# One fused attention and SSM kernel, the same tasks issued in another searched order

## The chip, the cores and the metric

The kernel runs on one core of a Trainium2 chip. The metric is device microseconds of one execution. TensorE is called PE here, its weight loads PEld, VectorE DVE, ScalarE ACT, GpSimd POOL and SyncE SP, as in the profile.

## The reference

Two branches over the same input `x` of 2048 positions and 640 channels, mixed by a gate:

```python
g = sigmoid((x * gate_w).sum(-1, keepdims=True))
a = attention(x, wqkv, wo)     # 32 heads of 20; 8 keys a position, 2 apart, backwards; softmax over 8
b = ssm(x, A, B, C, dt, Dskip) # K[d,l] = Re sum_n C*dB*exp(dt*A*l), y = causal conv(K, x) + x*Dskip
return g * a + (1 - g) * b
```

The convolution is done by FFTs in the reference and by matmuls with constant tables in the kernel.

## The kernel before

All work is cut into tasks. `Plan.add` makes a list of them; each has a name, the engines that can do it (`P` PE, `A` ACT, `D` DVE, `S` SP's DMA queue, `G` POOL's DMA queue; `AD` means ACT or DVE), and what it depends on. There are two plans, `main` (1295 tasks) and `tail` (304). `Plan.order` reads a string of numbers: each is the step to the next task's index in the list, and a letter behind it chooses the engine where there is a choice. `Plan.emit` issues the tasks in this order and chains each engine's instructions in it, so that an engine never overtakes: a task that waits holds all that stand behind it on its engine or queue. Data dependencies, the reuse of buffers and semaphores are worked out from the program, whatever the order is.

The task names, in the order in which the work flows:

- Parameters: `wr`, `tau`, `lin_t1` and the like on DVE and ACT, `mk0` to `mk9` pieces, `sp0` to `sp9` their stores, then `L0` to `L9`: loads of the SSM parameters for the ten chunks of kernel taps (L732; `L0` half on SP, half on POOL).
- Input: `turn`/`tev` transpose `x` (L207, eviction L473 on ACT or L475 on DVE). `late0` to `late59` are the projections to q, k and v (L291), `lev` their evictions, `lst<sc><w>` the stores to DRAM of quarter `sc` (w: 0 q, 1 k, 2 v; L307).
- Attention in eight pieces of 256 positions: loads `qc`, `kc` (L330) and `vc` (L339), both on POOL; `prod` (DVE, L345) and `lg` (PE, L351) make logits; `max`, `neg`, `exp`, `sum`, `at` the softmax (`exp` on ACT needs the Exp table); `ast` and `asb` send the weights through DRAM on SP; `pv` (DVE, L415) and `gat` (PE, L422) apply them, `oT` evicts; `wo` (PE, L446) projects, `ga` evicts with the gate (ACT L455, DVE L457), `gaS` stores on SP.
- Kernel taps in ten chunks `c`, three units each: `arg` (PE, L767), `act` (ACT: Sin L782, Exp L784), `pq`, `pqb`, `pqc` (DVE, L804 and L806), `kmm` (PE, L822, many short matmuls), `fin<c>` evicts the chunk. After chunk 4 and chunk 9 the taps are expanded: `shift`, `own`, `other` on DVE, `move` and `near`, stores `xst`, loads `xld` (L904, on SP and POOL).
- First FFT stage: `f1`, `fu`, `fk` matmuls (L1266, L1285) and their evictions `f1e`, `fue`, `fke` (some `fke` in halves `h0`, `h1`). `fu` reads `Usb`, which `rows0` to `rows7` load on POOL (L970); between two of them POOL copies two elements into `pace` (L969) when the earlier has landed. The buffer of `Usb` is that of the projections' staging tile, so `rows0` waits until all `lst` of quarters 1 to 3 have landed. `gates` loads the gate (`omF`, L973).
- Tail: `fp`/`sp` second FFT stage, `ta`, `tc`, `Y` the product on DVE, `inv`/`cp` inverse, `yp` then `tt`+`mx` or `st` the last stage with the mix, `out` the stores.

The function tables: an ACT task with a table (`exp`, `ln`, `sin`, `atan`) behind one with another needs an `ACT_TABLE_LOAD`.

Of the kernel before, what the change touches and what calls it, by code (L numbers as in the profile page):

```python
# [38 lines left out]
def _attn_consts():  # L39
# [10 lines left out]


ORDER = {"main": (
# [41 lines left out]
), "tail": (  # L94
# [8 lines left out]
)}  # L103


# [1259 lines left out]
```

## Time and profile before

| | us |
|---|---|
| median of 3 runs (339.92 to 340.62) | 340.38 |
| profiled execution, first to last instruction | 339.6 |
| busy: PE, DVE, ACT, POOL | 289.5, 298.9, 290.2, 92.3 |

The profiled execution is given by its span, 339.6 us; the median of the runs stands 0.8 us above it. Busy times say how long an engine worked on something; a busy PE is not PE at its peak. The views used below: busy time of each engine in stretches; groups of instructions by line, engine and shape (busy time in all, mean ns of one, idle time before them and what ended it); waits (who waited for whom); and the timeline, one row an instruction or a few merged ones (start, duration, engine, line, operation, tiles out<-in).

### The profile page before, as it was taken

The page shows a single profiled execution, that of the slowest core. Times are in us where ns is not written, and L with a number is a line of the kernel's source. Part 1 is how long each engine was busy: PE and PEld are TensorE (multiplying, and loading weights), DVE is VectorE, ACT ScalarE, POOL GpSimd, SP SyncE. Part 2 cuts the span into 40 slices and gives each one's busy share as a digit, 9 for nine tenths or more (in the row PEclk, how much of TensorE's full clock was granted, in tenths as well). Part 3 has the DMA queues.
Part 4 walks back from the last instruction along what each step waited for, and adds up shares of the span by engine and source line. Part 5 has one row for each costly group of instructions (what it writes and reads, how often), then busy time and mean ns, then how long its engine had stood idle before and what let it go on. Part 6 is the DMA issues. An engine that isn't in the chain of part 4 may idle for free. (4 is left out here: it accounts for less than half of the span.)

```text
span 339.6 us, 12013 instructions
## 1 busy us (share of the span) xinstructions
PE 289.5 (85%) x5181; PEld 172.1 (51%) x5214; DVE 298.9 (88%) x407; ACT 290.2 (85%) x424; POOL 92.3 (27%) x119
## 2 busy tenths in 40 slices
PE   0699999999997899999999979669999899996760
PEld 0446544444453455455545444445765676665750
DVE  3999988789998799999899989786888979999982
ACT  1899737999997899999999998786976779998991
POOL 8603334041052161102137615621130000000053
PEclk9999999999998999999999999997999999999996
DMA  7997854378279781285738585982882336576056
GB/s 251 356 259 233 222 131 133 103 207 166 66 195 249 186 204 38 42 233 161 252 58 206 124 224 129 207 187 50 235 281 93 124 113 198 139 142 118 2 136 177
DMA packets 48949, 56.30 MB, mean 166 GB/s; under 512 B 25498, under 2 KB 40154, under 8 KB 48898
## 3 DMA queue, kind: packets, MB, share of 16 engines
q1 hardware_dynamic: 39928, 27.90, 31.2%
q0 software_dynamic: 8224, 27.04, 30.2%
q8 instruction: 40, 0.66, 0.8%
q10 hardware_dynamic: 746, 0.61, 0.5%
q14 instruction: 11, 0.09, 0.1%
HBM read 36.26 MB, written 19.27 MB: 164 GB/s over the span
## 5 line engine op out<-in xcount | busy, mean ns | idle before, releaser
L291 PE MATMUL tb<-bufA 128*128 128x512 bf16 x267 | 73.3, 389 | 5.0 <-issue 3.1
L782 ACT ACTIVATE big<-ar 128x740 bf16<-128x740 int16 (+1 forms) x72 | 56.1, 854 | 2.5 <-issue 1.2
L784 ACT ACTIVATE big<-ar 128x848 bf16<-128x848 f32 x60 | 50.3, 918 | 1.8 <-PE ar L767 1.8
L767 PE MATMUL ar<-Rarg,L 64*128 64x212 bf16 (+4 forms) x600 | 48.8, 253 | 3.5 <-ACT big L784 1.5
L345 DVE TENSOR_TENSOR prod<-qc,kc 128x2048 bf16<-128x2048 bf16 x40 | 47.8, 1218 | 4.2 <-PE lg L351 3.3
L415 DVE TENSOR_TENSOR pv<-vc,asb 128x2048 bf16<-128x2048 bf16 x40 | 48.2, 1217 | 0.9 <-PE tb L422 0.9
L291 PEld LDWEIGHTS <-bufA 128*128 128x128 bf16 x300 | 31.0, 122 | 28.0 <-issue 11.3
L822 PEld LDWEIGHTS <-pt 128*32 128x32 bf16 (+1 forms) x2560 | 25.8, 92 | 37.0 <-issue 34.4
L822 PE MATMUL kps<-qq,pt 128*32 128x21 bf16 (+1 forms) x2560 | 36.9, 173 | 8.0 <-issue 6.6
L804 DVE TENSOR_TENSOR pt<-big 128x1024 bf16<-128x1024 bf16 x48 | 33.3, 701 | 5.6 <-issue 2.0
L767 PEld LDWEIGHTS <-L 64*128 64x128 bf16 x600 | 20.6, 94 | 27.1 <-issue 23.4
L446 PE MATMUL tb<-wo_sb,oT 128*128 128x320 bf16 x160 | 28.6, 301 | 0.7 <-DVE ga L457 0.4
L1157 POOL DMA_DIRECT2D out_dram<-ot x14 | 7.7, 557 | 77.9 <-DVE ot L1139 77.9
L473 ACT ACTIVATE prj<-tb 128x512 bf16<-128x512 f32 x32 | 20.0, 632 | 8.8 <-PE tb L291 8.6
L422 PE MATMUL tb<-pv,ind 128*64 128x512 bf16 (+1 forms) x192 | 25.0, 363 | 2.5 <-issue 2.3
L473 ACT ACTIVATE sp_u<-fp 128x640 bf16<-128x640 f32 x31 | 23.9, 952 | 0.8 <-PE fp L1039 0.8
L473 ACT ACTIVATE sp_k<-fp 128x640 bf16<-128x640 f32 x29 | 22.6, 969 | 1.2 <-DMA PHX<-c_phi 1.0
L969 POOL COPY pace<-Usb 32x2 bf16<-32x2 bf16 x7 | 14.3, 2045 | 25.9 <-DMA Usb<-in_A_x_dram 25.9
L806 DVE TENSOR_TENSOR qq<-big 128x1344 bf16<-128x1344 bf16 x24 | 21.2, 883 | 0.0
L339 POOL DMA_DIRECT2D vc<-vS x16 | 11.9, 771 | 28.9 <-DVE pv L415 12.4
L1039 PEld LDWEIGHTS <-PHI 128*128 128x128 bf16 x160 | 15.5, 97 | 8.0 <-issue 1.0
L455 ACT ACTIVATE ga<-tb,g_sb 128x320 bf16<-128x320 f32 x26 | 13.8, 544 | 4.4 <-PE tb L446 3.0
(168 smaller groups left out, 562.4 us busy)
## 6 DMA issues: line engine op xcount, KB each, us to landing
vc<-vS POOLq DMA_DIRECT2D x16, 327.5 KB, 6.9
kc<-kS POOLq DMA_DIRECT2D x8, 337.5 KB, 6.1
xn<-in_A_x_dram SPq DMA_DIRECT2D x4, 640.0 KB
qc<-qS POOLq DMA_DIRECT2D x8, 320.0 KB, 5.9
gaS<-ga SPq DMA_DIRECT2D x8, 320.0 KB
Usb<-in_A_x_dram POOLq DMA_DIRECT2D x8, 320.0 KB, 5.1
gaF<-gaS SPq DMA_DIRECT2D x8, 320.0 KB
bufA<-in_A_wqkv_dram SPq DMA_DIRECT2D x3, 800.0 KB
```

The source lines that it names most:

```text
L291: nc.tensor.matmul(ppf, self.wq[:, which, kt, e::5], self.xT[:, c0 // 1024, kt, c0 % 1024:c0 % 1024 + SC], start=(kt == 0), stop=(kt == NK ...
L345: nc.vector.tensor_tensor(b[e][:], b["qc"][:, e, :].unsqueeze(1).to_broadcast([128, W, C]), win(b["kc"][:, e, :], 0, W, DIL, C), ALU.mult)
L415: nc.vector.tensor_tensor(o, vw, b["asb"][:].unsqueeze(2).to_broadcast(sh), ALU.mult)
L422: nc.tensor.matmul(b["op", e][64 * a:64 * a + 64, 0:n, :], ind[:, 32:96], b["pv", e][:, w, a, 0:n, :], start=(w == 0), stop=(w == 3), skip ...
L446: nc.tensor.matmul(apf[:, :320], b["oT"][:, e, i * 128:(i + 1) * 128], wo_sb[:, e, hf * 320:(hf + 1) * 320], start=(e == 0), stop=(e == 4))
L473: nc.scalar.activation(o, i, ACT.Identity)
L767: nc.tensor.matmul(ar[:, g2, a0:a0 + ncol], L[rows, sb, gv, l0:l0 + 128], R[rows, c0:c0 + ncol], start=True, stop=True, tile_position=(64 ...
L782: nc.scalar.activation(d_[:, :, s0 * QW:s1 * QW], ar[:].bitcast(I16)[:, :, 0:2 * (s1 - s0) * QW:2], ACT.Sin, scale=SCL)
L784: nc.scalar.activation(dst[:, gp::2].rearrange("p g s n -> p g (s n)"), ar[:, :, 0:2 * EW], ACT.Exp)
L804: nc.vector.tensor_tensor(pt[:, :, k, :], gg[:, :, ::-1] if k else gg, e1, ALU.mult)
L806: nc.vector.tensor_tensor(qq[:], trg[:, :, KI:].rearrange("p a (v m) -> p a v m", v=2), exq[:, :, KI:].unsqueeze(2).to_broadcast([128, 32, ...
L822: nc.tensor.matmul(kps[32 * g:32 * g + 32, h, NM * ql:NM * ql + NM], pt[rows, k, v, :], qq[rows, k, v, :], start=(g not in started), stop= ...
```

## The change

Both strings of `ORDER` are replaced; nothing else is. The title's search is the program that wrote the string; it is no part of the kernel. The diff, cut to the first and last numbers of each plan:

```diff
 ORDER = {"main": (
-    "52 -52 7 -4 -2 3 11 -4 -6 -3 51A -45 -2 6 48 1D -5 1A -44 41 1A 3 1A 13 -63 1 15 -2 61 -11 1D -60 2 69 1A -5 1 -4 1 "
...
+    "0 3 -1 4 1 1 1 1 5 10 -13 -11 3 24 1 29 1 -7 2 -1 2 5 -30 31 -5 1 15 1 11 -73 2 34 27 11 -80 83 -65 66 -3 4 1 1 -78 79 "
...
+    "-642 644 -1 -7 9D -8 15 1 -27 22 -21 11 11D -21 6 -5 6 4D 11 4 -24 25 -4D -19 -1 15 -13D 7 7 -37 31 -30"
 ), "tail": (
-    "3 1A 7 1A -7 1D 1 6 1A -6D 1 1A 10 -5 1A 1 1A 3 13 1D -13 1 1 2 1A 3 1A -3 1A -4 11 1A 6 -11 1A 11 -6 1A 1 1A -41 1 "
...
+    "3 -3 5 -1D 2D 5 1 -11 12 -11 5 1 7 -6 5D 3 21 -18 -4 -6D 11 13 -16 1 20 -13 9 -7 -1 9 -7 8 -15 1 7 -6 8 -1 -6 15 -7 20 "
```

Read against the list of tasks, the two orders differ as follows. Evictions that may run on either engine (DVE before, DVE after; the rest on ACT): `lev` 19, 17; `ga` 6, 11; `oT` 3, 6; `fue` 6, 2; `fke` 6, 5; `fin` 4, 2; `tev` 2, 1; `lin_t1` 0, 1; in the tail `sp` 4, 5. ACT's order in `main` changes its table 18 times before and 22 after; `exp0` and `exp3` now stand between Sin tasks of one chunk.

What stands ahead of `fin9`, the last chunk's eviction, and behind it in `main`, where the two orders differ:

| | ahead, before | ahead, after | behind, before | behind, after |
|---|---|---|---|---|
| DVE `pv` | 30 | 35 | 10 | 5 |
| DVE `ga`, `oT`, `lev` | 2, 0, 19 | 7, 3, 17 | 4, 3, 0 | 4, 3, 0 |
| DVE `fin`, `tev`, `lin_t1` | 3, 2, 0 | 1, 1, 1 | 0 | 0 |
| DVE `fue`, `fke`, `fke` halves | 0 | 0 | 6, 3, 3 | 2, 4, 1 |
| ACT table loads of the plan | 18 | 22 | 0 | 0 |
| ACT `fue`, `f1e` | 0, 9 | 6, 10 | 14, 1 | 12, 0 |
| ACT `ga`, `oT`, `lev` | 18, 16, 41 | 17, 17, 43 | 8, 5, 0 | 4, 1, 0 |
| ACT `fin`, `tev`, `lin_t1` | 6, 8, 1 | 8, 9, 0 | 0 | 0 |
| ACT `fke`, `fke` halves | 0 | 0 | 2, 7 | 1, 9 |

POOL's queue in the stretches that change most (each name waits for its data, and holds the ones behind it):

```
before: lst00 lst01 qc0 kc0 kc256 qc256 L0G lst11 consts kc512 lst10 ...
after:  lst00 lst01 kc0 qc0 qc256 L0G kc256 lst02 lst10 vc0 qc512 ...

before: ... xst0G lst22 rows0 rows1 qc1792 vc1024 rows2 kc1792 rows3 rows4 xld0G rows5 vc1280 rows6 vc1536 rows7 gates1 gates3 vc1792 xst1G ...
after:  ... xst0G xld0G lst32 lst22 rows0 vc1024 rows1 qc1792 kc1792 rows2 rows3 rows4 vc1280 rows5 rows6 rows7 gates3 gates2 gates1 gates0 vc1536 vc1792 xst1G ...
```

SP's queue, the main differences: `L2 ast1 asb0 L3 asb1` becomes `asb0 L2 ast1 L3 gaS0 asb1`; `L8 gaS1 ast4 asb4 L9 gaS2 ast5 xld0S` becomes `ast4 xld0S L8 ast5 gaS2 asb4 L9`; at the end of the tail the stores of the eight output pieces are issued in the order 1 0 2 3 4 7 6 5.

90 rows, old and new, of the table ORDER are left out of this document.

## The prediction

> **What bounds the kernel now.** First the page's head and busy shares, then the busy time of each engine in stretches cut where the work changes: loads and parameters, the projections, the joint stretch of attention and kernel chunks, the last chunk's end (`fin9` starts at 236.7), the end of the main plan (271.5), the tail.
>
> ```profile
> span 339.6 us, 12013 instructions
> PE 289.5 (85%) x5181; PEld 172.1 (51%) x5214; DVE 298.9 (88%) x407; ACT 290.2 (85%) x424; POOL 92.3 (27%) x119
> ...
> core 0: us, PE busy (x) PEld busy (x) DVE busy (x) ACT busy (x) POOL busy (x), PEclk, DMA share, GB/s
> 40.00:58.00 18.00, 17.09 (x104) 7.88 (x104) 15.16 (x23) 8.89 (x16) 5.94 (x9) 1.00 0.58 159
> 58.00:120.00 62.00, 57.00 (x1147) 27.81 (x1158) 54.34 (x73) 57.37 (x78) 15.73 (x20) 0.97 0.67 164
> 120.00:200.00 80.00, 74.16 (x1822) 39.35 (x1830) 77.12 (x108) 79.67 (x121) 28.96 (x31) 1.00 0.59 152
> 200.00:236.70 36.70, 29.93 (x808) 17.58 (x805) 30.59 (x40) 28.95 (x42) 13.21 (x17) 0.95 0.66 147
> 236.70:271.50 34.80, 32.12 (x248) 23.24 (x247) 30.62 (x43) 27.41 (x40) 3.84 (x7) 1.00 0.60 185
> 271.50:334.00 62.50, 51.59 (x832) 38.59 (x832) 57.61 (x88) 56.52 (x94) 7.07 (x13) 0.99 0.52 128
> ```
>
> No one engine is the bound. In 40 to 58 PE is (17.1 of 18), ACT idles 9.1. In 120 to 200 DVE and ACT are both full (77.1 and 79.7 of 80). In 200 to 236.7 ACT idles 7.8 and DVE 6.1, from 236.7 to 271.5 they idle 7.4 and 4.2: only there and in 40 to 58 is there slack that an order could take. The waits of 200 to 236.7 say why:
>
> ```profile
> PE kps L822 <- issue: 6.1, 4, 2.0
> ACT bufA L473 <- PE bp L1266: 3.2, 2, 2.7
> DVE pt L804 <- issue: 2.0, 1, 2.0
> ```
>
> PE stood 6.1 us in four waits for nothing but its own next instruction, amid the short `kmm` matmuls, and ACT and DVE then waited for PE.
>
> **The change part by part.** No task is added or dropped. Evictions change engine, ACT's order needs 22 switches of its function table instead of 18, and queues are permuted. I count what each engine has ahead of `fin9` and behind it, in both orders, and price the difference by these rows (busy, mean ns of one).
>
> ```profile
> L415 DVE TENSOR_TENSOR pv<-vc,asb 128x2048 bf16<-128x2048 bf16 x40 | 48.2, 1217 | 0.9 <-PE tb L422 0.9
> L473 ACT ACTIVATE big<-bp 128x1024 bf16<-128x1024 f32 x14 | 14.2, 1044 | 2.2 <-PE bp L1266 2.2
> L455 ACT ACTIVATE ga<-tb,g_sb 128x320 bf16<-128x320 f32 x26 | 13.8, 544 | 4.4 <-PE tb L446 3.0 <-ACT big L782 0.9 <-DMA gaS<-ga 0.4
> L475 DVE CAST big<-bp 128x1024 bf16<-128x1024 f32 x6 | 7.2, 1221 | 1.7 <-PE bp L1266 1.6
> L457 DVE TENSOR_SCALAR ga<-tb,g_sb 128x320 bf16<-128x320 f32 x6 | 3.2, 544 | 1.5 <-DMA gaS<-ga 1.3 <-PE tb L446 0.2
> L473 ACT ACTIVATE prj<-tb 128x512 bf16<-128x512 f32 x32 | 20.0, 632 | 8.8 <-PE tb L291 8.6
> L475 DVE CAST prj<-tb 128x512 bf16<-128x512 f32 x13 | 8.9, 686 | 3.5 <-PE tb L291 3.5
> L475 DVE CAST E<-kps 128x336 bf16<-128x336 f32 x4 | 2.0, 503 | 1.8 <-PE kps L822 1.8
> L782 ACT ACT_TABLE_LOAD x6 | 7.7, 1283 | 0.5 <-PE ar L767 0.4
> ```
>
> *Ahead of `fin9`, DVE*: 5 more `pv` (+6.1), 5 more `ga` (+2.7), 3 more `oT` (+1.8, priced as `prj` and a shorter one), 1 `lin` (+0.7, estimated as `prj`), 2 fewer `lev` (-1.4), 2 fewer `fin` (-1.0), 1 fewer `tev` (-1.2): +7.7. Successive instructions overlap: the pair of `pv` below takes 2.35, so the second adds 1.13, not 1.22. Nine net instructions at 0.08 less: **+7.0**. *ACT*: 4 table loads (+5.1), 6 more `fue` and 1 `f1e` (+7.3), 1 `tev` (+1.0), 2 `fin` (+1.0), 2 `lev` (+1.3), 1 `oT` (+0.6), less 1 `ga` and 1 `lin` (-1.6): +14.7, less 0.12 of overlap for twelve: **+13.2**. PE gains about 7 in matmuls of the same tasks; it had 6.8 idle in 200 to 236.7 alone and hides them. So `fin9` starts 7.0 later if DVE sets it (243.7) and 13.2 later if ACT does and fills no idle time (249.9). ACT can fill some: the loads around the first softmax (`exp0`, which now stands between two Sin tasks) fall at the end of the PE-bound stretch, about 1.5 of them in its 9.1 idle; the six `fue` stand in 200 to 236.7, where ACT idled 7.8, of which I take 3. That is 13.2 - 4.5 = 8.7: `fin9` at **245.4**.
>
> Here a rule weighs against the change. In the row each load takes 1283 ns with 0.5 us of idle time before all six, nothing like a second cost. The Trainium skill (ScalarE: Activation LUTs, "What ACT_TABLE_LOAD costs") adds a drain of about 1380 ns to each switch; by it four more switches would be 10.6 instead of 5.1 and the time at the end 343.3. The trace shows no such idle time, so the row decides, and that case gets 0.02 among the ACT-bound ones below.
>
> *Behind `fin9`, DVE*: 5 fewer `pv` (-6.1), 4 fewer `fue` (-4.9), 2 fewer half `fke` (-1.4), 1 more `fke` (+1.2): -11.2, with overlap **-10.3**. *ACT*: 4 `ga` (-2.2), 4 `oT` (-2.2), 2 `fue`, 1 `fke` and 1 `f1e` (-4.1) fewer, 2 halves more (+1.2): -7.3, with overlap **-6.0**. That leaves 20.3 on DVE and 21.4 on ACT of the 30.6 and 27.4 above. Then the chain from `fin9` through DRAM sets the end:
>
> ```profile
> 236.68 0.51 DVE L475 CAST E<-kps 128x336 bf16<-128x336 f32 x1 [1.76 <-PE kps L822]
> 239.59 0.76 DVE L869 COPY X<-nxt 128x80 bf16<-128x80 bf16 x3 [0.41 <-ACT nxt L473]
> 240.26 2.35 DVE L415 TENSOR_TENSOR pv<-vc,asb 128x2048 bf16<-128x2048 bf16 x2
> ...
> 246.15 0.56 POOL L904 DMA_DIRECT2D kc<-Kx  x1 [4.35 <-PE bp L1266]
> 248.71 0.38 SPq L904 DMA_DIRECT2D kc<-Kx  x1
> ...
> kc<-Kx POOLq DMA_DIRECT2D x2, 640.0 KB, 4.4
> ```
>
> `fin9` to the end of `other1` 3.7, plus one `oT` now between, 4.3; to the loads' issue 5.8 on POOL and 8.4 on SP (there `gaS5` stood ahead; now `gaS6` does), landing 4.4: 10.2 to 12.8, I take 11.5; then nine half `fke`, one whole and one `fue` on ACT, 6.5 with the first matmul. 22.3, against 21.4 of ACT work: **22.5**, or 27 if PE's ring waits cost again the 4 to 7 us idle of today. The tail has one `sp` eviction moved to DVE (0.7 either way) and its outputs reordered: 0, bounds 1 each way.
>
> *Queue positions.* On SP `asb0` moves ahead of `L2`, `xld0S` ahead of `L8`, and `gaS0` ahead of `asb1`. The first two wait for stores that are long issued when `L2` and `L8` may start. Behind `gaS0`, which waits for `ga011`, stand `asb1` and then `L4`; between `ga011` and the first `pv1` stand about seven `prod`-sized instructions of DVE, 8 us, for an issue and a landing: 0, bounds 0 and 2. On POOL two moves count. `kc256` moves behind the four `L0` loads:
>
> ```profile
> 47.63 2.59 POOL L732 DMA_DIRECT2D L<-Sprm  x4 [6.82 <-issue]
> ...
> 53.20 2.35 DVE L345 TENSOR_TENSOR prod<-qc,kc 128x2048 bf16<-128x2048 bf16 x2
> ...
> kc<-kS POOLq DMA_DIRECT2D x8, 337.5 KB, 6.1
> ```
>
> It was issued at 39; now at 50.2, landing at 56.3, while its `prod10` would start near 54.4 (two `lev` more ahead, one `prod` row as above): 0 to 1.9 lost in a PE-bound stretch; I take 1.0. The other is the rows chain, the first rival. *Renewals.* PE's waits for instructions (6.1) may shrink to nothing or be met elsewhere; bounds -6 and +6, taken 0, as the instructions and their number stay.
>
> **Sum.** The tail starts at 245.4 + 1.0 + 22.5 = 268.9 instead of 271.5: 339.6 - 2.6 = 337.0 of span. The median of the runs (340.38) stands 0.8 above this span: **337.8**. Bounds of the terms: 243.7 + 21 gives 333, 249.9 + 25 gives 343.
>
> **The rivals.** *First, the other side: the loads of the FFT's input come late.* `rows0` may start only when all projections are stored; the last eviction (`lev42`) now has 13.4 us more DVE work ahead (5 `prod`, 7 of the `pq` kind, 2 softmax pieces), so `rows0` is at 185.2.
>
> ```profile
> 171.76 0.80 POOL L970 DMA_DIRECT2D Usb<-in_A_x_dram  x1 [5.55 <-PE ar L767]
> 181.65 9.43 POOL L969 COPY pace<-Usb 32x2 bf16<-32x2 bf16 x1 [0.76 <-DMA Usb<-in_A_x_dram]
> 196.94 0.18 POOL L969 COPY pace<-Usb 32x2 bf16<-32x2 bf16 x1 [4.25 <-DMA Usb<-in_A_x_dram]
> 204.13 3.08 POOL L969 COPY pace<-Usb 32x2 bf16<-32x2 bf16 x1 [6.25 <-DMA Usb<-in_A_x_dram]
> 225.29 0.79 POOL L970 DMA_DIRECT2D Usb<-in_A_x_dram  x1
> 226.07 1.07 POOL L973 DMA_DIRECT2D omF<-omS  x2
> ...
> vc<-vS POOLq DMA_DIRECT2D x16, 327.5 KB, 6.9
> ```
>
> The eight loads took 53.5 from first to last issue, 11.7 of it two tiny pacing copies that took 9.43 and 3.08 (others about 0.4, 0.18 where DVE stood still). Without those 11.7 `rows7` is issued at 227.0, and `vc1536`, which stood ahead of it and now stands behind it and four small loads, lands 10.5 later (0.8 of its own issue, 2.1 of four `omF` loads, 0.7 of the first half, 6.9): 237.5. `pv60` has 1.1 more DVE work ahead than `fin9` had: 237.8. No margin is left. Held copies as in this trace make it 349 (337.8 + 11); half of them 343. It decides from 3.6 us of held copies on. For it: DVE stays nearly full there; against: ACT is the tighter engine there, and each DVE wait lets a copy through. By the Trainium skill (SBUF — State Buffer, "Who interferes with whom") a DVE instruction with two SBUF inputs blocks a GpSimd instruction that reads SBUF; the trace agrees (9.43 against 0.18).
>
> *Second, ACT becomes the bound*: nothing of the 13.2 is absorbed, 4.5 later: 342; with half absorbed 340.4, no change. *Third, the order removes the renewal stalls as well* (4 of the 6.1): 333.8. *Fourth, transfers and renewals were no cost and the orders are equal*: inside 340.4 ± 0.7.
>
> **How the numbers follow.** Forecast 337.8 (335.5 to 339.6): 0.42. Late rows, 341 to 349: 0.29. ACT-bound or equal, 339.7 to 343: 0.17, of which 0.13 within 0.2%. Better, 333 to 335.5: 0.12. This measurement tells a change from none at about 0.2% (0.7 us). Faster 0.42 + 0.12 = 0.54, same 0.13, slower 0.29 + 0.04 = 0.33. Range 333.0 to 346.0: it leaves out the far half of the late rows.
>
> **What would show it.** Right: 23 table loads on ACT, `fin9` near 245, the stretch from it to the tail's first `fp` 22 to 24 long, ACT idle in 40 to 58 below 9. Wrong: `pv60` waiting for `vc`, `fu8` waiting for `Usb` (rows chain); a first `fp` after 272; PE's instruction waits over 8 us.

## The result and the profile after

The changed kernel is not faster. In the first comparison it took 344.25 us (median of 4 executions, 342.08 to 345.49) beside 340.5 of the kernel before: a ratio of 1.0107 [1.0058, 1.0157]. Two later comparisons gave medians of 343.38 beside 342.6, ratio 1.0022 [0.997, 1.0073], and 342.6 beside 341.8, ratio 0.9901 [0.9844, 0.9957]. A ratio leaves disturbed executions out, and where few are left (three of twelve in the third comparison, four of thirteen for the changed main with the tail of before below) it can stand against its own medians. So means of all executions are given too. All 28 executions of the changed kernel have a mean of 342.8 us (standard error 0.5), 104 of the kernel before 342.2 (0.2): the difference is +0.2%, one to two standard errors, where -0.8% was forecast.

First the head of the page and the busy time in the same stretches as before (columns: us, then busy us and instructions of PE, PEld, DVE, ACT, POOL, the granted clock, DMA):

```profile
span 340.0 us, 12021 instructions
PE 287.1 (84%) x5188; PEld 174.5 (51%) x5214; DVE 296.4 (87%) x407; ACT 296.9 (87%) x428; POOL 89.4 (26%) x119
...
core 0: us, PE busy (x) PEld busy (x) DVE busy (x) ACT busy (x) POOL busy (x), PEclk, DMA share, GB/s
40.00:58.00 18.00, 16.14 (x164) 8.24 (x164) 15.11 (x23) 10.57 (x15) 5.53 (x8) 1.00 0.64 197
120.00:200.00 80.00, 69.20 (x1718) 37.58 (x1718) 72.77 (x105) 77.15 (x112) 18.97 (x28) 0.97 0.62 158
200.00:236.70 36.70, 33.67 (x895) 21.32 (x894) 31.85 (x40) 34.98 (x51) 19.62 (x19) 0.98 0.56 121
236.70:271.50 34.80, 29.65 (x279) 21.87 (x279) 26.71 (x40) 26.04 (x36) 2.82 (x5) 0.90 0.64 203
271.50:334.00 62.50, 50.90 (x824) 37.66 (x821) 57.96 (x87) 56.03 (x93) 6.00 (x11) 0.98 0.51 118
```

The slack of 200 to 236.7 and of 40 to 58 is used (ACT idles 1.7 instead of 7.8, and 7.4 instead of 9.1). But 120 to 200, full on DVE before (77.1), now has 72.8. The waits say why:

```profile
DVE pv L412 <- DMA vc<-vS: 4.4, 1, 4.4
DVE prod L342 <- DMA kc<-kS: 4.0, 1, 4.0
...
PE kps L819 <- issue: 0.5, 1, 0.5
```

PE's waits for its own instructions around 200 to 240 fell from 6.1 to 0.5 in this execution. In their place DVE waits twice for a load. The queue that issues these loads, POOL's:

```profile
180.30 0.81 POOL L967 DMA_DIRECT2D Usb<-in_A_x_dram  x1 [5.36 <-PE ar L764]
...
185.11 0.60 POOL L966 COPY pace<-Usb 32x2 bf16<-32x2 bf16 x1 [2.58 <-DMA Usb<-in_A_x_dram]
185.66 0.79 POOL L967 DMA_DIRECT2D Usb<-in_A_x_dram  x1
186.56 0.88 POOL L327 DMA_DIRECT2D qc<-qS  x1
187.42 0.88 POOL L327 DMA_DIRECT2D kc<-kS  x1
...
203.84 5.15 POOL L966 COPY pace<-Usb 32x2 bf16<-32x2 bf16 x1 [3.71 <-DMA Usb<-in_A_x_dram]
...
226.01 3.34 POOL L966 COPY pace<-Usb 32x2 bf16<-32x2 bf16 x1 [4.89 <-DMA Usb<-in_A_x_dram]
...
232.08 2.16 POOL L336 DMA_DIRECT2D vc<-vS  x3
```

and the DVE instructions that wait for them, with `fin9` (the eviction `E<-kps`) behind:

```profile
195.12 1.22 DVE L342 TENSOR_TENSOR prod<-qc,kc 128x2048 bf16<-128x2048 bf16 x1 [3.99 <-DMA kc<-kS]
...
239.15 3.50 DVE L412 TENSOR_TENSOR pv<-vc,asb 128x2048 bf16<-128x2048 bf16 x3 [4.45 <-DMA vc<-vS]
...
246.00 0.51 DVE L472 CAST E<-kps 128x336 bf16<-128x336 f32 x1 [0.62 <-PE kps L819]
```

`kc1792` is the `kc` issued at 187.42, behind `rows0`, its landing and `rows1`; its first `prod` (`prod70`) stands idle from 191.1 to 195.1. `vc1536` is among the three issued from 232.08 on.

The tail starts 1.5 us earlier than before and ends later: its own last part is longer. ACT's `tt` run breaks for 0.98 us and the last two `mx` come at its very end (after, then before):

```profile
321.59 2.20 ACT L1133 ACTIVATE tt<-yp,om 128x320 bf16<-128x320 f32 x5 [0.78 <-PE yp L1127]
324.77 7.21 ACT L1133 ACTIVATE tt<-yp,om 128x320 bf16<-128x320 f32 x17 [0.98 <-PE yp L1127]
...
332.21 1.05 DVE L1136 TENSOR_TENSOR ot<-tt,gaF 128x640 bf16<-128x640 bf16 x2
...
333.55 2.18 POOL L1154 DMA_DIRECT2D out_dram<-ot  x4 [1.42 <-DVE ot L1136]
```

```profile
323.00 9.30 ACT L1136 ACTIVATE tt<-yp,om 128x320 bf16<-128x320 f32 x22 [0.78 <-PE yp L1130]
...
332.45 2.18 POOL L1157 DMA_DIRECT2D out_dram<-ot  x4 [0.69 <-DVE ot L1139]
```

### The profile page after: what moved, and what is told of

The parts are those of the page before. It is cut to its first block, busy times and chain, and to the rows that moved or that the text cites. A ratio compares the mean times of both kernels' runs of the same rounds, so it can differ in the third digit from the quotient of the medians.

```text
span 340.0 us, 12021 instructions
## 1 busy us (share of the span) xinstructions
PE 287.1 (84%) x5188; PEld 174.5 (51%) x5214; DVE 296.4 (87%) x407; ACT 296.9 (87%) x428; POOL 89.4 (26%) x119
## 5 line engine op out<-in xcount | busy, mean ns | idle before, releaser
L288 PE MATMUL tb<-bufA 128*128 128x512 bf16 x274 | 72.1, 385 | 3.3 <-issue 1.4
L288 PEld LDWEIGHTS <-bufA 128*128 128x128 bf16 x300 | 32.0, 120 | 28.9 <-issue 9.4
L764 PEld LDWEIGHTS <-L 64*128 64x128 bf16 x600 | 21.6, 94 | 38.5 <-issue 35.7
L801 DVE TENSOR_TENSOR pt<-big 128x1024 bf16<-128x1024 bf16 x48 | 32.4, 704 | 2.1 <-ACT big L781 1.6
L819 PEld LDWEIGHTS <-pt 128*32 128x32 bf16 (+1 forms) x2560 | 23.0, 92 | 12.5 <-issue 11.5
L819 PE MATMUL kps<-qq,pt 128*32 128x21 bf16 (+1 forms) x2560 | 27.9, 175 | 1.2 <-issue 0.8
L419 PE MATMUL tb<-pv,ind 128*64 128x512 bf16 (+1 forms) x192 | 23.9, 360 | 4.6 <-DVE pv L412 4.5
L443 PEld LDWEIGHTS <-oT 128*128 128x128 bf16 x160 | 14.6, 100 | 10.6 <-issue 5.9
L470 ACT ACTIVATE big<-bp 128x1024 bf16<-128x1024 f32 x18 | 17.8, 1029 | 1.5 <-PE bp L1263 1.4
L966 POOL COPY pace<-Usb 32x2 bf16<-32x2 bf16 x7 | 11.5, 1644 | 27.2 <-DMA Usb<-in_A_x_dram 27.2
```

The lines of the kernel that those rows point to most:

```text
L288: nc.tensor.matmul(ppf, self.wq[:, which, kt, e::5], self.xT[:, c0 // 1024, kt, c0 % 1024:c0 % 1024 + SC], start=(kt == 0), stop=(kt == NK ...
L419: nc.tensor.matmul(b["op", e][64 * a:64 * a + 64, 0:n, :], ind[:, 32:96], b["pv", e][:, w, a, 0:n, :], start=(w == 0), stop=(w == 3), skip ...
L443: nc.tensor.matmul(apf[:, :320], b["oT"][:, e, i * 128:(i + 1) * 128], wo_sb[:, e, hf * 320:(hf + 1) * 320], start=(e == 0), stop=(e == 4))
L470: nc.scalar.activation(o, i, ACT.Identity)
L764: nc.tensor.matmul(ar[:, g2, a0:a0 + ncol], L[rows, sb, gv, l0:l0 + 128], R[rows, c0:c0 + ncol], start=True, stop=True, tile_position=(64 ...
L801: nc.vector.tensor_tensor(pt[:, :, k, :], gg[:, :, ::-1] if k else gg, e1, ALU.mult)
```

## The experiments

Theories: **late loads** (DVE waits for `kc1792`, or for `vc1536`, which is the prediction's first rival), **the tail's end**, **ACT's table loads**, **the pacing copies**, and **the clock alone**. Each kernel was timed beside the kernel before on the same chip. The names of tasks stand for their numbers in `ORDER`.

**The changed kernel again, and the POOL queue put right**

```diff
 # POOL's queue in the changed main order
+qc1792 kc1792
 lst22 rows0 vc1024 rows1
-qc1792 kc1792
 rows2 rows3 rows4 vc1280 rows5
+vc1536
 rows6 rows7
+vc1792
 gates3 gates2 gates1 gates0
-vc1536 vc1792
```

> The changed kernel as it is, for a second trace and more times. The first trace has two half-clock stretches of 6.8 us each where the kernel before had two of 3.4, a wait of 4.4 us of DVE for vc (pv60) and one of 4.0 for kc (prod70), and a span only 0.4 above that of before, though its runs lie 2 to 5 us above. Late transfers (POOL queue): both waits stand in this trace again, 3 to 8 us together. Clock: the half-clock stretches are again about 6.8 us long and this trace is 342 to 344 of time. If the waits are mostly gone and the time is the same, neither of the two transfers is the cause.

> The changed order with four loads moved in POOL's queue alone: qc1792 and kc1792 ahead of lst22 (they stood behind rows1), vc1536 ahead of rows6 and vc1792 ahead of the gates (they stood behind rows7 and the gates). Late transfers: prod70 and pv60 no longer wait (0 instead of 4.0 and 4.4), the time falls by 3 to 7 us against the changed kernel, to 337 to 341. Rival, ACT is the bound: its work is as before, so DVE's gain is idle time elsewhere and the time falls by under 1.5. Rival, the rows come later in turn and fu8 waits: no gain, PE waits for Usb.

Unchanged: 343.38 us, 1.0022 [0.997, 1.0073]. With the four loads first: 338.81 (336.41 to 342.99), 0.991 [0.9864, 0.9957], and no wait for `kc` or `vc` in its trace. A change of the POOL queue alone takes 1.1%.

**The two plans apart**

> The main plan of after with the tail's order of before. In the first trace the tail starts 1.5 us earlier than before and its last output is issued 1.1 later (last mx at 332.5 against 331.4, last POOL store at 333.6 against 332.5). Tail theory: 1.5 to 2.5 us faster than the changed kernel, 341.5 to 343. Rival, the main plan alone is to blame: within 0.7 of the changed kernel.

> The main plan of before with the tail's order of after. Tail theory: 1.5 to 2.5 us slower than before, near 342.5. Rival, the main plan alone is to blame: within 0.7 of before, near 340.4. The two tail kernels together should add up to the whole difference of 3.7 us.

The changed main with the tail of before: 341.42, 0.9867 [0.9802, 0.9932], a ratio of four executions; all 13 have a mean of 341.6 (standard error 1.1) beside 342.9 (0.7) of the changed kernel in the same comparison. The main of before with the changed tail: 342.24, 1.005 [0.9994, 1.0106]; all 12 have 342.0 (0.4) beside 342.6 (0.4) of the kernel before. So these two runs do not yet show which tail is better; for the changed main the runs on the tail's end below do, for the main of before it stays open. The second run also shows what one profile is worth: this is the main order of before unchanged, and its timeline has `fin9` at 231.7 instead of 236.7; its waits have 1.7 us of `kmm` matmuls waiting for instructions where the profile of before has 6.6.

```profile
231.68 0.51 DVE L476 CAST E<-kps 128x336 bf16<-128x336 f32 x1 [0.66 <-PE kps L823]
```

```profile
PE kps L823 <- issue: 1.7, 2, 1.4
```

**Which load, and both causes together.** The edit of each is the named part of the diff above.

> The changed kernel with only qc1792 and kc1792 moved, ahead of lst22. prod70 waited 4.0 to 4.7 us for kc in three profiles of the changed main order, pv60 0.3 to 4.4 us for vc. If the wait for kc is the loss: prod70 waits 0, the ratio to before is 0.990 to 0.994. If the wait for vc is the loss, or DVE only makes up the 4 us in a later wait: 0.999 to 1.005, and pv60 waits for vc more than before.

> The changed kernel with only vc1536 moved ahead of rows6 and vc1792 ahead of gates3. pv60 then waits 0 for vc. If this wait (the first rival of the prediction) is the loss: 0.990 to 0.995. If the wait of prod70 for kc is the loss: 0.999 to 1.005, with prod70 still waiting 4 us. Both may give half each: 0.995 to 0.999.

> The changed main order with qc1792, kc1792, vc1536 and vc1792 issued earlier on POOL, and the tail order of before. If the late loads and the end of the tail are separate losses, their gains add: 1.1% (the loads) and 0.5 to 1.5% (the tail) off the changed kernel, a ratio to before of 0.980 to 0.986. If the tail's order is no cost and what differed was the clock, 0.989 to 0.993, as with the loads alone.

Only `qc1792` and `kc1792` first: 338.65, 0.9902 [0.9862, 0.9942], as much as all four. Only the two `vc`: 341.04, 1.0013 [0.9974, 1.0053], none. In the first one's timeline `kc1792` (171.82) is issued 16 us earlier, `prod70` (193.00) starts without a wait, and `fin9` at 242.9; in the second one's waits `prod70` still stands 3.7 us:

```profile
170.95 0.88 POOL L330 DMA_DIRECT2D qc<-qS  x1
171.82 0.88 POOL L330 DMA_DIRECT2D kc<-kS  x1
...
193.00 1.22 DVE L345 TENSOR_TENSOR prod<-qc,kc 128x2048 bf16<-128x2048 bf16 x1
...
242.92 0.50 DVE L475 CAST E<-kps 128x336 bf16<-128x336 f32 x1
```

```profile
DVE prod L345 <- DMA kc<-kS: 3.7, 1, 3.7
```

The move also clears POOL's queue for the rows (`rows7` is issued at 220.8 instead of 229.3), but that is not the gain: without the pacing copies, below, `rows7` is issued at 202.1 and nothing is gained, and in no trace does PE wait for `Usb`.

All four loads first and the tail of before: 336.14 (334.51 to 337.91), 0.9845 [0.9807, 0.9883]. It beats both kernels.

**The same edit in the kernel before**

```diff
 # POOL's queue in the main order of before
+qc1792 kc1792
 lst22 rows0 rows1
-qc1792
 vc1024 rows2
-kc1792
 rows3
```

> The kernel before with the same one edit that the changed kernel gained 1.2% from: qc1792 and kc1792 ahead of lst22. prod70 waited only 0.9 to 1.0 us for kc there. If the gain is this wait: 0.997 to 1.000. If an earlier kc helps in any order (by clearing POOL's queue for rows0 to rows7): 0.988 to 0.994.

It is slower, 347.5, 1.0129 [1.0069, 1.0189], which neither theory expected. Its timeline shows how, and two rows of the timeline of before, `lst22` and `vc1024`, what moved:

```profile
170.49 0.85 POOL L331 DMA_DIRECT2D qc<-qS  x1 [7.10 <-DVE prod L346]
...
172.21 0.87 POOL L308 DMA_DIRECT2D vS<-prj  x1
178.61 0.80 POOL L971 DMA_DIRECT2D Usb<-in_A_x_dram  x1 [5.53 <-PE ar L768]
...
192.75 1.43 POOL L340 DMA_DIRECT2D vc<-vS  x2
...
202.36 1.23 DVE L416 TENSOR_TENSOR pv<-vc,asb 128x2048 bf16<-128x2048 bf16 x1 [6.11 <-DMA vc<-vS]
```

```profile
165.39 0.82 POOL L307 DMA_DIRECT2D vS<-prj  x1 [2.96 <-ACT prj L473]
...
179.43 1.46 POOL L339 DMA_DIRECT2D vc<-vS  x2 [1.32 <-issue]
```

`qc1792` waits until a `prod` of an earlier piece gives its buffer free, at 170.5. Behind it now stands `lst22` (172.2 instead of 165.4), so `rows0` comes at 178.6 instead of 171.8, `vc1024` at 192.8 instead of 179.4, and DVE waits 6.1 us for it. In the changed order the two loads were issued at 171.0 and 171.8 too, but `lst22`, which waits there for a later eviction, was not held by them: `rows0` came at 182.1, as in the second trace of the changed kernel. An early place is good only where the load can be issued at once.

**Pacing**

```diff
-            nc.gpsimd.tensor_copy(P["pace"][32 * g0:32 * g0 + 32, :], P["Usb"][32 * g0:32 * g0 + 32, 32 * h0, 0:2])
+            pass
```

> The changed kernel without the seven copies into pace: rows1 to rows7 no longer wait for the earlier load, and no POOL copy stands in the queue. kc1792 is then issued about 2.3 us behind rows1 without the 4.6 us of pacing ahead of it. If pacing (its waits and held copies) makes kc and vc late: prod70 and pv60 wait under 1 us, ratio to before 0.989 to 0.994. If the loads then contend with kc, vc and the expansion's own transfers, they land as late as now: 0.998 to 1.008.

342.04, 0.9993 [0.9949, 1.0036]: no difference from the changed kernel. In its trace (an execution at a mean clock of 0.956) `kc1792` is issued 3.9 us behind `rows0` instead of 7.1, among other loads in flight, and `prod70` waits as long:

```profile
DVE prod L345 <- DMA kc<-kS: 4.0, 1, 4.0
DVE pv L415 <- DMA vc<-vS: 2.8, 1, 2.8
```

So taking the pacing copies out gains nothing; in this trace, with more loads in flight together, `kc1792` took 10.3 us from issue to landing instead of 7.6.

**ACT's table loads**

```diff
 # main order, beside the four loads first
-act00000 act00001 ... exp0 ...
+exp0 act00000 act00001 ...
-... act3121None act30000 ... act30101 ... exp3
+lg33 lg34 max3 ... neg3 act3121None exp3 act30000 ... act30101
```

> The four loads first, the tail as changed, and exp0 and exp3 no longer between two Sin tasks: act00000 and act00001 go behind exp0, exp3 (with lg33, lg34, max3, neg3) ahead of act30000. Four table loads fewer, 19 in all, 5.1 us of ACT. If ACT sets fin9 and the loads aren't absorbed, fin9 comes 5 us earlier than with the loads first alone (241.8) and the ratio to before falls from 0.991 to 0.976 to 0.980. If half is absorbed, as the prediction took, 0.983 to 0.986. If DVE sets it, 0.990 to 0.993.

> The four loads first, the tail of before, and exp3 (with lg33, lg34, max3, neg3) ahead of act30000 instead of between two Sin tasks: two table loads fewer, 2.6 us of ACT where ACT is busy over 96%. If ACT's table loads in the full stretch set fin9, the ratio falls from 0.9845 to 0.977 to 0.981. If DVE or PE set it, or the order around it loses what the loads give, 0.982 to 0.988. If ahead of this stretch ACT was not the loss in the run with four loads fewer, but this move, 0.990 or more.

19 loads instead of 23 is slower than the loads first alone: 343.47, 1.0027 [0.9986, 1.0068] against 0.991. The move of `exp0` empties ACT where it had something to do. In the timeline it waits 4.7 us for `neg0`; in the windows PE, which waits for ACT's Sin tasks, is busy 1.4 of 3.4 us, and the stretch behind has half the clock:

```profile
53.96 0.60 ACT L375 ACTIVATE at<-lg 128x512 bf16<-128x512 f32 x1 [4.66 <-PE lg L371]
```

```profile
53.10:56.51 3.41, 1.41 (x6) 0.52 (x5) 2.56 (x5) 2.52 (x3) 0.83 (x1) 1.00 0.64 225
56.51:59.92 3.41, 2.91 (x20) 1.33 (x20) 0.41 (x1) 2.50 (x4) 2.31 (x3) 0.51 0.70 220
```

Moving `exp3` alone, with the tail of before: 337.01, 0.9879 [0.9832, 0.9926], against 0.9845 without: no gain from 2.6 us less of ACT, though ACT is busy 98% of 120 to 200 in the run without this move. Fewer table loads brought no time in either edit. That they cost nothing isn't shown, as both edits also move other tasks: in the second one's trace a `pv` now waits 2.1 us for `vc`, and why the run with 19 is slower by 1% is only partly in the rows above (behind them, at `exp1`, it is 1.7 us late).

**The tail's end**

> The four loads first and the changed tail, but its end (yp, tt, mx, st, out) in the order of before. With the tail of before as a whole the ratio was 0.9845, with the changed tail 0.991; from cp19 to the end of the span the changed end takes 19.4 to 19.9 us in all traces but one, the end of before 17.6 to 18.2. If the end alone is the difference: 17.6 to 18.2 again and a ratio of 0.983 to 0.987. If the earlier part of the tail (one sp on DVE, the order of the first evictions) is: 0.989 to 0.993.

> The changed main order with qc1792 and kc1792 ahead of lst22 as its only edit, and the tail of before. If the late kc and the end of the tail are the whole of what the forecast missed, this does as well as with all four loads moved (0.9845): 0.982 to 0.988. If vc1536's and vc1792's places matter after all: 0.988 to 0.992.

> The changed kernel with two edits: qc1792 and kc1792 ahead of lst22, and in the tail's end tt4 ahead of tt5 on ACT and mx4 ahead of mx5 on DVE. In the changed tail tt5 stands ahead of tt4 and waits about 1 us for yp5, which comes behind one of PE's waits for instructions. If this swap is the tail's loss: cp19 to the end 18 to 18.6 us and a ratio 0.3 to 0.5% under that of the first edit alone (0.990), 0.985 to 0.987. If st6 behind mx7 and tt8, mx8 last are the loss: 19 us or more, 0.988 to 0.992.

> The changed kernel unchanged, on the same chip as the two above, so that their ratios can be set beside its own. It gave 1.011 and 1.002 in two comparisons: 1.000 to 1.010 expected, with prod70 waiting about 4 us for kc.

Loads first, and only the end (`yp`, `tt`, `mx`, `st`, `out`) as before: 336.69, 0.9865 [0.9821, 0.9909], as good as the whole tail of before (0.9845 [0.9807, 0.9883]) within the intervals; its `tt` run has no break:

```profile
316.94 9.35 ACT L1136 ACTIVATE tt<-yp,om 128x320 bf16<-128x320 f32 x22 [0.78 <-PE yp L1130]
...
326.44 2.18 POOL L1157 DMA_DIRECT2D out_dram<-ot  x4 [0.69 <-DVE ot L1139]
```

The two causes alone undone (`kc` first, tail of before): 337.38, 0.9883 [0.9824, 0.9943]; as far as was forecast (0.9924) or further. Its interval meets that with four loads moved (0.9845), so the places of the two `vc` are worth nothing that can be told here. The single swap of `tt4` and `tt5`: 340.5, 0.9916 [0.9869, 0.9963], no better than `kc` first alone (0.9902). Its trace says otherwise: the `tt` run has no break, though PE waits 0.9 us for its instructions between two `yp`, and from the last eviction of `cp` to the end of the span it takes 18.0 us, as was expected if the swap is the loss. So whether it is stays open. The third comparison of the changed kernel stands in the result.

Worked out from the timelines (us; renewal waits are PE's `kps` and `ar` waits for "issue" in the whole span, the tail starts with its first `fp` matmul, the end runs from the end of the last eviction of `cp` to the end of the span; the expectations above have this end 0.2 to 0.4 longer):

| kernel | wait for kc, vc | renewal waits | `fin9` | `fin9` to tail | end | span |
|---|---|---|---|---|---|---|
| before | 0.9, 0 | 6.6 | 236.7 | 35.0 | 17.4 | 339.6 |
| before, tail changed | 1.0, 0 | 1.7 | 231.7 | 35.0 | 19.4 | 337.9 |
| before, kc first | 0, 6.1 | 3.9 | 241.3 | 35.1 | 17.8 | 344.8 |
| changed | 4.0, 4.4 | 0.8 | 246.0 | 24.1 | 19.1 | 340.0 |
| changed, again | 4.2, 0.3 | 3.2 | 243.5 | 23.3 | 19.4 | 336.9 |
| changed, third | 3.4, 0 | 3.7 | 247.8 | 23.4 | 18.1 | 340.0 |
| only vc first | 3.7, 0 | 5.4 | 245.7 | 23.3 | 19.2 | 338.9 |
| only kc first | 0, 0 | 5.9 | 242.9 | 23.4 | 17.9 | 335.0 |
| kc first, `tt4` and `tt5` swapped | 0, 0 | 6.2 | 248.0 | 23.4 | 18.0 | 341.5 |
| four loads first | 0, 0 | 5.8 | 242.0 | 23.5 | 19.7 | 337.1 |
| four loads, end of before | 0, 0 | 3.9 | 241.0 | 23.5 | 17.7 | 333.9 |
| four loads, tail of before | 0, 0 | 5.6 | 241.4 | 24.1 | 17.8 | 334.0 |
| kc first, tail of before | 0, 0 | 4.9 | 243.2 | 23.5 | 18.1 | 335.4 |

The ratios differ from comparison to comparison by as much as one cause is worth (the unchanged changed kernel had 1.011, 1.002 and 0.990), so here are the means of all executions:

| kernel | executions | mean us (standard error) | mean clock |
|---|---|---|---|
| before, of the four later comparisons | 100 | 342.2 (0.2) | 0.971 |
| changed | 28 | 342.8 (0.5) | 0.970 |
| only vc first | 12 | 342.0 (0.6) | 0.971 |
| kc first or all four loads first, end as changed (three kernels) | 32 | 339.5 (0.4) | 0.974 |
| kc first or all four loads first, end or tail of before (three kernels) | 18 | 336.9 (0.3) | 0.977 |

They point the same way as the ratios: the early `kc1792` is worth 3.3 us, the end of before beside it another 2.7, and the places of the two `vc` nothing clear of the noise. The clock alone is no explanation: the changed kernel and the kernel before have the same mean clock. By the 2.7 us for 0.01 of mean clock that the last section gives, about 1 us of each of the two gains goes with a higher clock (an estimate).

## Why the prediction was wrong, by its own steps

The forecast was faster by 0.8%; measured was no gain. With two edits in it the order does gain as much as was forecast (0.9883), but two terms that the sum held at nothing took that back. That this comes so near is in part luck: its span, 335.4, is made of other terms than the 337.0 of the sum, as the points on `fin9` show.

- **Queue positions, the step that failed.** "On POOL two moves count" was wrong: a third did. `kc1792` is issued earlier than before (187.4 against 191.8), so it didn't look like a loss; but its reader moved further. `prod70` could have started at 197.0 before, as its row in the timeline of before shows (0.89 before 197.94), and at 191.1 after:

```profile
197.94 1.22 DVE L345 TENSOR_TENSOR prod<-qc,kc 128x2048 bf16<-128x2048 bf16 x1 [0.89 <-DMA kc<-kS]
```

  A load is late against its reader, not against its old place. The reader came 5.9 us earlier, the load only 4.4, and it also took 7.6 us from issue to landing instead of 6.1: so the wait grew from 0.9 to 4.0. The sum had neither. Price: 3.3 us (1.0%) by the means, 1.2% by the ratios, beside waits of 3.4 to 4.2 in the three traces; shown by undoing it alone.
- **First rival, the rows chain.** What it described is there: held copies of 5.15 and 3.34 us (the forecast feared 11.7 in all), `vc1536` issued at about 232 and `pv60` waiting 4.4. But in the next two traces that wait was 0.3 and 0, and giving the two `vc` early places changed no time. That the measured times lie in the band of this rival (341 to 349) is luck: another load's wait took them there. As this wait was hardly there in two of the three traces, what 4.4 us of it would cost isn't shown.
- **The tail: 0 (bounds 1 each way).** In seven of ten traces with the changed end it takes 19.1 to 19.7 us from the last eviction of `cp` on, against 17.4 to 18.1 in all seven with the end of before: 1.0 to 2.3 more. In the other three it takes 17.9 to 18.1: in two PE did not wait for its instructions between two `yp`, in one `tt4` and `tt5` were swapped. Such a wait of PE (1.0 to 1.1 us) stands in the traces with the end of before too, without a break in `tt`. So the reordered outputs cost time when this wait comes. Undoing the end alone moved the ratio from 0.991 to 0.9865 and the mean from 338.9 to 337.0; the intervals overlap, the traces and the 18 executions above are clearer.
- **Ahead of `fin9`: 245.4, and 1.0 for `kc256`.** Measured 246.0, 243.5 and 247.8 in the three traces: about right in value, but with the wait for `kc` inside it. Without that wait it is 241.0 to 243.2 in five of the six traces in the table (248.0 in the sixth, at a mean clock of 0.959). So in the five not 4.5 of ACT's 13.2 us but 6.7 to 8.9 were absorbed against the base of 236.7, and 1.7 to 3.9 against the other profile of the same order (231.7). `prod10` did not wait for `kc256` at all.
- **Behind `fin9`: 22.5.** Measured to the tail's first `fp` it is 23.3 to 24.1 in the ten traces of the changed main order in the table, 35.0 to 35.1 in the three of the order before. The mechanism is right, the term 0.8 to 1.6 too small.
- **Renewals: 0, bounds 6.** They are no property of the order: 0.8 to 6.2 us with the changed main order in the table, 1.7 to 6.6 with the old one. The third rival (they vanish) looked true in the first trace and is gone in the next. The sum was made against a profile that had drawn the highest value in the table.
- **Span to time: 0.8.** The time is 1.7 to 3.0 us above the span in every execution that gave both, 1.9 in the median. The 0.8 set the span of one execution beside the median of others; the sum of 337.0 was a time of 338.9. The bounds that were added up, 333 and 343, are spans as well, times of about 335 and 345.
- **Second rival, ACT as the bound:** not seen; two and four table loads fewer gave nothing, though both edits moved other tasks as well.

Of what was to show it, 23 table loads, `fin9` near 245, ACT's idle time in 40 to 58 (7.4) came as written, and the tail's first `fp` before 272; the stretch behind `fin9` was 24.1 in the first trace and 23.3 and 23.4 in the next two, at the upper end of 22 to 24, and `pv60` did wait for `vc`, as the list of wrong signs had it. The decisive sign, `prod70` waiting for `kc`, was on no list.

## What to carry to other kernels

When an order is changed, list for every load its issue and its landing against the new start of its first reader, not against its old place in the queue; a load that moved earlier can still be late. An earlier place pays only where the load can be issued at once: one that waits for its buffer holds the whole queue, and the same edit gained about 1% in one order and lost 1.3% in the other. And take the base of a sum from several profiles: random waits of one execution (5 us here) are as large as what is forecast.

## What the runs showed of the hardware

TensorE's granted clock falls to half in stretches of 3.41 us or two or three such, and these follow stretches of 3.41 us in which PE was little busy. The windows of the changed kernel, around DVE's wait for `kc` and around its wait for `vc`, cut on the clock's own grid (PE's busy time follows the length; PEclk is the third number from the end):

```profile
188.07:191.48 3.41, 3.29 (x37) 1.50 (x37) 2.99 (x6) 3.41 (x7) 0.41 (x2) 1.00 0.94 268
191.48:194.90 3.42, 2.13 (x84) 1.28 (x80) 0.00 (x0) 3.42 (x6) 0.81 (x1) 1.00 1.07 250
194.90:198.31 3.41, 1.99 (x11) 0.90 (x10) 3.19 (x4) 2.84 (x3) 0.00 (x0) 0.51 0.48 79
235.88:239.30 3.42, 1.41 (x10) 1.12 (x10) 0.15 (x1) 2.65 (x3) 0.00 (x0) 1.00 1.01 195
239.30:242.71 3.41, 1.73 (x7) 0.72 (x7) 3.41 (x4) 0.00 (x0) 0.00 (x0) 0.50 0.53 80
```

While DVE waits, PE starves (2.13 and 1.41 of 3.42), and the stretch behind runs at half clock: a wait can be paid a second time. Over all 17 traces, from 45 to 316 us, cut on this grid, with PE's busy share worked out from the matmuls:

| PE busy in a stretch at full clock | stretches | next one at half clock |
|---|---|---|
| under 0.5 | 32 | 31 |
| 0.5 to 0.6 | 20 | 7 |
| 0.6 to 0.7 | 46 | 4 |
| over 0.7 | 1200 | 0 |

The Trainium skill (TensorE: Matmul & The Clock Gate, "What's actually happening") has the window of 3413 ns and the half rate behind an idle one; the traces agree on the length, but here half a window of idleness was enough. The mean clock of an execution and its time go together (about 2.7 us for 0.01 among the executions of one kernel), and so the scatter of 1% from run to run, of the kernel before too (336.87 to 348.66), would fit PE's short waits for its instructions, which differ from trace to trace and can draw half-clock stretches behind them; that they are its source isn't shown. How much of a lost microsecond is the wait and how much the clock was not separated.
